# First queries' norms taken beside K's, paired bound rows, and one query product spread over the first scores of an attention and GEGLU block

## The chip, the cores and the metric

The kernel runs on one core of a Trainium2 chip. The metric is device time in microseconds (us) of one execution. An execution that the hardware profiler took lies beside the timed runs; its rows are what is read below. Times in rows count from the first instruction of the span.

The engines are called as in the profile: PE is TensorE's matmuls and PEld its weight loads, DVE is VectorE, ACT is ScalarE, POOL is GpSimd, SP is SyncE. A q behind a name (SPq, ACTq) marks the issuing of a DMA.

## What is computed

One transformer block over 2048 tokens of width 512. There are 32 query heads of width 16, and all of them share one K and one V head. All arrays are float32.

```python
def _A_ref(x, wq, wk, wv, wo):
    q = (x @ wq).reshape(B, S, H, Dh).transpose(0, 2, 1, 3)
    k, v = x @ wk, x @ wv
    scores = einsum("bhqd,bkd->bhqk", q, k) * (Dh ** -0.5)
    o = einsum("bhqk,bkd->bhqd", softmax(scores), v)
    return o.transpose(0, 2, 1, 3).reshape(B, S, H * Dh) @ wo
def _B_ref(x, w_gate, w_up, w_down):
    return (gelu(x @ w_gate) * (x @ w_up)) @ w_down
h = x + _A_ref(layernorm(x), wq, wk, wv, wo)
return h + _B_ref(layernorm(h), w_gate, w_up, w_down)
```

## The kernel before

**Precision.** Every float32 factor of a projection is split into a high and a low part (`split`), and a product is three matmuls: high by high, high by low, low by high. A score uses the same idea inside one matmul: its contraction has 50 rows, which are 16 rows of K's high part, 16 and 16 of the other combinations, and two rows that carry an upper bound of the score. The bound replaces the row maximum of the softmax.

**Blocks.** The tokens are four blocks of 512 (`T`). A block's queries are four chunks (`c`) of 128 columns, that is 8 heads each. A projection of one chunk, `pq_<block>_<chunk>`, is 12 matmuls of 128 x 512 in one PSUM bank. Attention runs over block, group of 4 heads (`g`) and 16 key chunks of 128 tokens (`kc`). A key chunk has two steps, counted by `n`: each step is one pair of score matmuls (two heads, on the upper and the lower 64 rows of PE) into a two-bank tile `s`, and one exponential `p` of 128 x 1024 on ACT. After both steps of a key chunk `weigh` multiplies `p` with V into `acc`; that is 4 matmuls in the program, which the trace shows as 8.

**Prologue.** It normalizes and transposes x, projects K and V for all four blocks (`project_k`), and starts on block 0's queries. Chunk 0 (`q_first`) is finished early, since the first group of heads needs it; chunks 1 to 3 (`q_rest`) are a generator of 36 matmuls that `advance` moves on by a number of matmuls. K's largest norm `k2m` comes from four small products `pkn` with a reduction each on DVE (`norm_k`, `max_k`). The queries' norms `pqn` come from one product, which DVE copies to `qn` and reduces. From `k2m` and the queries' norms POOL works out two factors (`mm`), ACT makes the bound `m`, and `first_bound` sends its rows to `qg_first`.

**The first queries' tile.** `qg_first` holds the 4 heads of the first group twice: on rows 0 to 49 and on rows 64 to 113. `first_q` brings the half that the first eight steps use, from DRAM (`q_d`). `fill_first` brings the crossed half on POOL's queue. The crossed half is first used at step 8 (`START`), where score matmuls begin to run beside half-array matmuls of the next blocks' projections and so swap sides.

**K's low part and V.** For each block ACT copies K and V out of PSUM (`add_k`, `leave_k`, which makes `vT`), POOL subtracts to get K's low rows (`low_k`), PE transposes V (`turn_v`) and DVE copies it into place (`leave_v`). `vT` and the plain copies of a query product, `pq_raw`, share one tag with 3 buffers.

**Order.** PE, POOL and ACT run in the order in which the code is written, in attention as in the prologue; so does DVE in the prologue and up to the last projection, and SP from `first_bound` on. Each engine is strictly in order. So a query product that is written in front of the first scores is done in front of them, and a copy that waits holds up what is written behind it on its engine. `HURRY` lists the chunks that are first copied out of PSUM as they are (`pq_raw`) and split later.

**After step 8.** Each stretch of steps is interleaved with the projections of blocks 1 to 3 (`later_q`), with the splitting of the dense weights on POOL (`part_weights`), and later with the output projection and the GEGLU products (`dense`, `weave`). The order of all that is fixed by step numbers.

Of the kernel before, what the change touches and what calls it, by code (L numbers as in the profile page):

```python
# [9 lines left out]
F32 = mybir.dt.float32  # L10
# [30 lines left out]
HURRY = ((0, 3), (1, 0), (1, 1))  # L41
# [21 lines left out]
def kernel(  # L63
# [104 lines left out]
    def run(outer, first):  # L168
# [20 lines left out]
        if first:  # L189
            eb = early.enter_context(tc.tile_pool(name="early", bufs=1))  # L190

            xT = {}
            for b in range(1, NB):
                for w in ("hi", "lo"):
                    if (b, w) in IN_RING:
                        part = ring_tile(f"xT_{w}_{b}").rearrange("p f i d -> p (f i) d")
                    else:
                        part = eb.tile([P, DC, T], F32R, name=f"xT_{w}_{b}")
                    xT.setdefault(b, []).append(part)
            wq_hi = eb.tile([P, DC, D], F32R, name="wq_hi")  # L200
            wq_lo = eb.tile([P, DC, D], F32R, name="wq_lo")
            sel = eb.tile([P, DC, H], BF16, name="sel")
            k2m = eb.tile([H, 1], F32, name="k2m")


        def project_q(b, cs, eng, col, whole=None):
# [6 lines left out]
            for c in cs:  # L213
# [134 lines left out]
        def first_q():  # L348
# [3 lines left out]
            for a in range(2):  # L352
                for r0, r1 in ((3 * DH + 1, KR), (0, 3 * DH)):
                    nc.sync.dma_start(
                        qg[64 * a + r0 : 64 * a + r1, a::2, :].bitcast(F32),
                        view[r0:r1, a:4:2, :T].bitcast(F32),
                    )
            return qg

        def fill_first(qg):  # L360

            view = q_d.rearrange("h r s -> r h s")
            for r0, r1 in ((0, 3 * DH), (3 * DH + 1, KR)):
                for a in range(2):
                    nc.gpsimd.dma_start(
                        qg[64 * a + r0 : 64 * a + r1, 1 - a :: 2, :].bitcast(F32),
                        view[r0:r1, 1 - a : 4 : 2, :T].bitcast(F32),
                    )
            m = ms[0]
            for j in range(4):  # L370
                row = 64 * (1 - j % 2) + 3 * DH
                nc.gpsimd.dma_start(
                    qg[row : row + 1, j, :].bitcast(F32), m[j : j + 1, :].bitcast(F32)
                )

        def first_bound(qg):

            m = ms[0]
            for u in range(2):
                for a, eng in enumerate((nc.sync, nc.scalar)):  # L380
                    eng.dma_start(
                        qg[64 * a + 3 * DH : 64 * a + 3 * DH + 1, 2 * u + a, :].bitcast(F32),
                        m[2 * u + a : 2 * u + a + 1, :].bitcast(F32),
                    )
# [10 lines left out]
        if first:  # L395
# [3 lines left out]
            with order:  # L399
                qg_first = prologue(  # L400
                    psum1, xT, wq_hi, wq_lo, sel, k2m, q_first, q_rest, advance,
                    first_q, first_bound, fill_first, eb
# [671 lines left out]
        with tc.manual_schedule(engines={mybir.EngineType.SP, mybir.EngineType.DVE}):  # L1074
            parts = None
            if first:
                work = later_q()
                parts = part_weights(early.enter_context(tc.tile_pool(name="parts", bufs=1)))

            token, left, wo_due = None, 6 * (NB - 1) * DC * DC, True  # L1080
            while n < lead:
# [166 lines left out]
    def prologue(psum1, xT, wq_hi, wq_lo, sel, k2m, q_first, q_rest, advance, first_q, first_bound, fill_first, eb):  # L1248
        with ExitStack() as pro:
            sb = pro.enter_context(tc.tile_pool(name="pro", bufs=1))  # L1250
            xT[0] = [sb.tile([P, DC, T], F32R, name=f"xT_{w}_0") for w in ("hi", "lo")]
# [203 lines left out]
            advance(q_first, 2)  # L1455
# [4 lines left out]
            for b in range(NB - 2, NB):  # L1460
                add_k(b, pks[b])
                vTs[b] = leave_k(b, pks[b])
# [3 lines left out]
            with tc.manual_schedule(engines={mybir.EngineType.SP}):  # L1466
# [4 lines left out]
                fill_first(qg)  # L1471
                for b in range(2, NB):
# [94 lines left out]
```

## Time and profile before

| | us |
|---|---|
| median of 3 runs | 1411.42 |
| lowest and highest of them | 1409.36 and 1412.17 |
| the profiled execution | 1409.89 |
| its span | 1408.1 |
| PE busy in it | 1391.7 (99%) |
| ACT busy in it | 1041.2 (74%) |
| DVE and POOL busy in it | 552.7 (39%) and 189.4 (13%) |

A busy PE is no proof that PE is the limit, because matmuls are pipelined and their ends are modelled. What counts is the stage. The prologue ends and attention begins at about 51 us in the span, so the change lies in the stretch from about 38 to 61 us. The chain of waits, the timelines of single engines and the table by stretches show what ends last there.

### The profile page before, as it was taken

To read this page: it belongs to the slowest core of one execution; us is meant where nothing else is said; L and a number is where in the kernel's file an instruction comes from. 1 tells how busy PE (TensorE), PEld (TensorE's weight loads), DVE (VectorE), ACT (ScalarE), POOL (GpSimd) and SP (SyncE) were. 2 spreads that over 40 slices of the span, in tenths; PEclk is the share of its full clock that TensorE was granted. 3 is DMA by queue.
4 is the path that set the end of the run, shared out by engine and by line. 5 is a ranking of instruction groups with operands and counts; after the bars stand their busy time and mean duration, and the time that the engine had idled before them with its cause. 6 is when DMAs were issued, how large, how long until landed. Compare 5 with 4: busy or idle time off the path is not lost.

```text
span 1408.1 us, 25648 instructions
## 1 busy us (share of the span) xinstructions
PE 1391.7 (99%) x10646; PEld 782.7 (56%) x10646; DVE 552.7 (39%) x982; ACT 1041.2 (74%) x1149; POOL 189.4 (13%) x288
## 2 busy tenths in 40 slices
PE   8999999999999999999999999999999999999998
PEld 7433333335555555555555655555555555557886
DVE  7322323333342434333252433424352342427665
ACT  7699999996777787777787777777787777772000
POOL 6655565501000000000000000001000000002000
PEclk9999999999999999999999999999999999999999
DMA  4578777842341322233252332223242241335551
GB/s 160 162 238 273 236 243 243 298 134 91 126 150 53 124 106 102 73 112 122 84 169 72 117 118 87 87 100 111 99 151 97 88 147 56 134 124 198 181 199 59
DMA packets 85041, 194.52 MB, mean 138 GB/s; under 512 B 9904, under 2 KB 24240, under 8 KB 84884
## 3 DMA queue, kind: packets, MB, share of 16 engines
q1 hardware_dynamic: 77484, 167.39, 35.3%
q0 software_dynamic: 7264, 25.30, 5.0%
q8 instruction: 86, 1.41, 0.4%
q14 instruction: 39, 0.32, 0.1%
q10 hardware_dynamic: 168, 0.10, 0.0%
HBM read 142.93 MB, written 49.55 MB: 137 GB/s over the span
## 4 chain that ended last, share of the span: by engine, by line
PE 93%; ACT 3%; DMA 1%; issue 1%; DVE 1%; POOL 0%; SPq 0%; ACTq 0%; DVEq 0%; POOLq 0%
PE acc L439 33%; PE s L431 19%; PE pu L949 9%; PE pg L949 8%; PE pd L949 4%; PE pq L429 4%; PE pd L626 3%; ACT p L435 3%; PE pd L648 3%; PE pg L648 3%; PE pu L648 3%; PE pp L626 2%; PE pp L757 1%; DMA x<-in_A_x_dram 1%; PE pxt L693 1%
## 5 line engine op out<-in xcount | busy, mean ns | idle before, releaser
L435 ACT ACTIVATE p<-s 128x1024 f32<-128x1024 f32 x1024 | 969.7, 1030 | 224.6 <-PE s L431 220.1
L439 PE MATMUL acc<-p,v_sb 128*32 128x512 f32 x4096 | 496.4, 600 | 0.0
L431 PE MATMUL s<-qg,kaug 50*128 50x512 f32 x1984 | 416.3, 423 | 3.7 <-ACT p L435 3.6
L431 PEld LDWEIGHTS s<-qg,kaug 50*128 50x128 f32 x1984 | 194.6, 184 | 217.8 <-ACT p L435 120.6
L439 PEld LDWEIGHTS acc<-p,v_sb 128*32 128x32 f32 x4096 | 109.8, 109 | 229.2 <-issue 226.0
L949 PE MATMUL pu<-x2h,w 64*128 64x512 f32 x672 | 211.8, 391 | 0.0
L949 PE MATMUL pg<-x2h,w 64*128 64x512 f32 x672 | 211.5, 391 | 0.1
L949 PEld LDWEIGHTS pu<-x2h,w 64*128 64x128 f32 x672 | 115.8, 185 | 15.1
L949 PEld LDWEIGHTS pg<-x2h,w 64*128 64x128 f32 x672 | 116.2, 185 | 12.6 <-DVE g L823 0.5
L949 PE MATMUL pg<-x2l,w 64*128 64x512 f32 x336 | 122.2, 391 | 0.0
L949 PE MATMUL pu<-x2l,w 64*128 64x512 f32 x336 | 121.8, 390 | 0.0
L826 ACT ACTIVATE ga<-ga 128x512 f32<-128x512 f32 x56 | 35.3, 634 | 89.2 <-DVE ga L821 89.2
L139 POOL TENSOR_SCALAR rstd<-mv 128x1 f32<-128x1 f32 x16 | 3.5, 221 | 666.4 <-DVE mv L137 666.4
L949 PE MATMUL pd<-w,gh 64*128 64x512 f32 x384 | 81.3, 392 | 0.0
L891 DVE TENSOR_TENSOR h<-h,pd 128x512 f32<-128x512 f32 x48 | 31.9, 685 | 115.4 <-PE pd L949 66.4
L1192 DVE SCALAR_TENSOR_TENSOR ga<-ga,g 128x512 f32<-128x512 f32 x70 | 48.3, 691 | 52.3 <-ACT ga L826 51.2
L452 DVE COPY oT<-acc 128x512 f32<-128x512 f32 x32 | 22.1, 692 | 112.1 <-PE acc L439 111.9
L479 DVE RECIPROCAL oc<-oc 128x128 f32<-128x128 f32 x64 | 56.3, 921 | 24.3 <-DMA oc<-acc_d 19.5
L810 DVE COPY g<-pg 128x512 f32<-128x512 f32 x56 | 38.8, 692 | 62.8 <-PE pg L949 57.0
L949 PEld LDWEIGHTS pu<-x2l,w 64*128 64x128 f32 x336 | 57.9, 185 | 7.6
L949 PEld LDWEIGHTS pg<-x2l,w 64*128 64x128 f32 x336 | 58.1, 185 | 6.1
L823 DVE SCALAR_TENSOR_TENSOR g<-g,pu 128x512 f32<-128x512 f32 x56 | 38.2, 683 | 40.4 <-PE pu L949 30.4
(248 smaller groups left out, 1462.4 us busy)
## 6 DMA issues: line engine op xcount, KB each, us to landing
w<-w_d SPq DMA_DIRECT2D x112, 512.0 KB
w<-w_d SPq DMA_DIRECT2D x28, 1024.0 KB
qg<-q_d SPq DMA_DIRECT2D x46, 200.0 KB
q_d<-qh SPq DMA_DIRECT2D x32, 256.0 KB
wo<-wo_d SPq DMA_DIRECT2D x8, 1024.0 KB
acc_d<-oT SPq DMA_DIRECT2D x31, 256.0 KB
oc<-acc_d SPq DMA_DIRECT2D x124, 64.0 KB
w_d<-w_0b POOLq DMA_DIRECT2D x14, 512.0 KB, 7.6
```

Of the source, the lines that this page charges most:

```text
L429: step()
L431: nc.tensor.matmul(s[:, a, :], kaug[rows, kc * P : (kc + 1) * P], qg[rows, 2 * u + a, :], start=True, stop=True,)
L435: nc.scalar.activation(p[:, 2 * u : 2 * u + 2, :], s, AF.Exp, scale=SCALE)
L439: nc.tensor.matmul(acc[32 * j : 32 * j + 32, :], v_sb[:, kc, :], p[:, j, :], start=(kc == 0), stop=(kc == KC - 1), skip_group_check=True,)
L479: nc.vector.reciprocal(oc[:, 1, sl], oc[:, 1, sl])
L626: nc.tensor.matmul(banks[k], lhsT[rows], rhs[rows], start=(turn == 0 and i == 0), stop=(turn == 1 and i == n - 1), skip_group_check=True,)
L648: nc.tensor.matmul(bank, lhsT, rhs, start=(i == 0), stop=(i == len(ts) - 1))
L810: nc.vector.tensor_copy(g, pg)
L823: nc.vector.scalar_tensor_tensor(g, g, 0.5, pu, op0=ALU.mult, op1=ALU.mult)
L826: nc.scalar.activation(a, a, AF.Tanh, scale=GELU_A * GELU_C)
L949: nc.tensor.matmul(e["bank"], lhsT[rows], rhs[rows], start=i == 0 and not e["both"], stop=last and e["both"], skip_group_check=True,)
L1192: (soon or lazy).pop(0)()
```

## The change

Three things are moved and one form of transfer is changed.

First, `pqn` and its two DVE instructions go between the norm products of K's blocks 1 and 2. They stood between those of blocks 2 and 3. The transposes of V move too: block 1's goes in front of K's last norm product, and those of blocks 2 and 3 go behind chunk 1's product.

Second, the bound rows of `qg_first` go two heads at a time: one transfer on SP and one on ACT where there were two each, and two on POOL's queue where there were four. POOL's constant rows come with the first transfers of SP. On POOL the subtraction for K's block 2 now stands between the crossed half's queries and its bound rows.

Third, chunk 3's product of block 0 is put between the first scores: 3 matmuls after step 1, 6 after step 3, 3 after step 5. For that block 0's transposed x (`xT[0]`) moves to a pool of its own, which is closed after step 5; the pool for splitting weights opens there, too. Chunk 2 is now the one that ACT copies as it is, and DVE does its split and chunk 3's copy.

```diff
-HURRY = ((0, 3), (1, 0), (1, 1))
+HURRY = ((0, 2), (0, 3), (1, 0), (1, 1))
...
-                    if b == 0:
+                    if (b, c) == HURRY[0]:
                         nc.scalar.activation(raw, pq, AF.Copy)
                     else:
                         nc.vector.tensor_copy(raw, pq)
...
+        def bound_rows(qg, a, side, queue):
+            row = 64 * side + 3 * DH
+            queue.dma_start(
+                qg[row : row + 1, a::2, :].bitcast(F32), ms[0][a:4:2, :].bitcast(F32)
+            )
...
-            for u in range(2):
-                for a, eng in enumerate((nc.sync, nc.scalar)):
-                    eng.dma_start(
-                        qg[64 * a + 3 * DH : 64 * a + 3 * DH + 1, 2 * u + a, :].bitcast(F32),
-                        m[2 * u + a : 2 * u + a + 1, :].bitcast(F32),
-                    )
+            for a, queue in enumerate((nc.sync, nc.scalar)):
+                bound_rows(qg, a, a, queue)
...
-                if first and n == 2:
+                if first and n in (2, 4):
+                    advance(q_rest, 6)
+                if first and n == 6:
                     for _ in q_rest:
                         pass
+                    x0.close()
+                    parts = part_weights(early.enter_context(tc.tile_pool(name="parts", bufs=1)))
...
+                if c == 1:
+                    advance(q_first, 2)
             b = NB - 1
             ks = square_k(b, pks[b])
-            advance(q_rest, 3)
+            pv = turn_v(1, vTs[1])
+            add_k(b - 1, pks[b - 1])
+            vTs[b - 1] = leave_k(b - 1, pks[b - 1])
             max_k(b, norm_k(b, ks))
...
                 fill_first(qg)
-                for b in range(2, NB):
-                    low_k(b, vTs[b])
-                advance(q_rest, 12)
-                for b in range(1, NB):
-                    leave_v(b, turn_v(b, vTs[b]))
-                advance(q_rest, 3 * DC * (DC - FIRST_Q) - 21)
+                low_k(2, vTs[2])
+                for a in range(2):
+                    bound_rows(qg, a, 1 - a, nc.gpsimd)
+                low_k(3, vTs[3])
+                advance(q_rest, 6)
+                leave_v(1, pv)
+                for b in range(2, NB):
+                    leave_v(b, turn_v(b, vTs[b]))
+                advance(q_rest, 12)
```

What follows are the instructions as they stand on single engines; numbers behind a name tell its instances apart. On PE, before, chunk 3's product (`pq_3`) ends in front of the first six pairs of scores (`s`):

```order
L223 MATMUL pq_3_781<-xT_hi_106,wq_hi 128x512
L223 MATMUL pq_3_781<-xT_lo_107,wq_hi 128x512
L223 MATMUL pq_3_781<-xT_hi_106,wq_lo 128x512
L431 MATMUL s_0_816<-qg_first,kaug 128x512 x2
L431 MATMUL s_1_820<-qg_first,kaug 128x512 x2
L431 MATMUL s_0_834<-qg_first,kaug 128x512 x2
L431 MATMUL s_1_838<-qg_first,kaug 128x512 x2
```

On PE in the changed kernel chunk 2's product (`pq_2`) ends there, and chunk 3's first matmuls follow the second pair:

```order
L226 MATMUL pq_2_756<-xT_hi_101,wq_lo 128x512
L432 MATMUL s_0_788<-qg_first,kaug 128x512 x2
L432 MATMUL s_1_792<-qg_first,kaug 128x512 x2
L226 MATMUL pq_3_805<-xT_hi_101,wq_hi 128x512
L226 MATMUL pq_3_805<-xT_lo_102,wq_hi 128x512
L226 MATMUL pq_3_805<-xT_hi_101,wq_lo 128x512
L432 MATMUL s_0_810<-qg_first,kaug 128x512 x2
L432 MATMUL s_1_814<-qg_first,kaug 128x512 x2
```

Twelve matmuls of 128 x 512 have moved from in front of the first score to between the first and the seventh pair.

On POOL, before, the factors end, K's block 1 is subtracted, and all transfers of the crossed half are issued in one go, ahead of the subtractions of blocks 2 and 3:

```order
L299 TENSOR_SCALAR mm_0_677<-mm_0_677,k2m 32x1
L1379 TENSOR_TENSOR kaug<-vT_651,kaug 16x512 x2
L365 DMA qg_first<-q_d 48x2x512 x2
L365 DMA qg_first<-q_d 1x2x512 x2
L372 DMA qg_first<-m_0_678 1x16x32 x4
L1379 TENSOR_TENSOR kaug<-vT_688,kaug 16x512 x2
L1379 TENSOR_TENSOR kaug<-vT_691,kaug 16x512 x2
```

On POOL in the changed kernel:

```order
L302 TENSOR_SCALAR mm_0_671<-mm_0_671,k2m 32x1
L1382 TENSOR_TENSOR kaug<-vT_654,kaug 16x512 x2
L369 DMA qg_first<-q_d 48x2x512 x2
L1382 TENSOR_TENSOR kaug<-vT_690,kaug 16x512 x2
L377 DMA qg_first<-m_0_672 1x2x512 x2
L1382 TENSOR_TENSOR kaug<-vT_696,kaug 16x512 x2
```

Four short transfers are gone from POOL's queue, and the two that carry bound rows stand behind one subtraction more.

On ACT, before, between the bound `m` and the first exponential `p`:

```order
L323 ACTIVATE m_0_678<-qn_0_674,mm_0_677 32x512
L381 DMA qg_first<-m_0_678 1x16x32 x2
L127 ACTIVATE qh_2_772<-pq_2_738 128x512
L242 ACTIVATE pq_raw_3_794<-pq_3_781 128x512
L435 ACTIVATE p_815<-s_0_816 128x1024
```

On ACT in the changed kernel:

```order
L326 ACTIVATE m_0_672<-qn_0_668,mm_0_671 32x512
L377 DMA qg_first<-m_0_672 1x2x512
L245 ACTIVATE pq_raw_2_769<-pq_2_756 128x512
L436 ACTIVATE p_787<-s_0_788 128x1024
```

One transfer and one copy of 128 x 512 have left ACT in front of the first exponential; the copy that is left is chunk 2's. From step 8 on, the order of all engines is the same as before.

More of the change, by code (lines that the diff above doesn't have):

```diff
@@ L203, in run @@
             k2m = eb.tile([H, 1], F32, name="k2m")
+            x0_pool = x0.enter_context(tc.tile_pool(name="x0", bufs=1))
+            xT[0] = [x0_pool.tile([P, DC, T], F32R, name=f"xT_{w}_0") for w in ("hi", "lo")]
         def project_q(b, cs, eng, col, whole=None):
@@ L1245, in run, with prologue @@
         late.close()
-    def prologue(psum1, xT, wq_hi, wq_lo, sel, k2m, q_first, q_rest, advance, first_q, first_bound, fill_first, eb):
+    def prologue(psum1, xT, wq_hi, wq_lo, sel, k2m, q_first, q_rest, advance, first_q, first_bound, fill_first, bound_rows, eb):
         with ExitStack() as pro:
             sb = pro.enter_context(tc.tile_pool(name="pro", bufs=1))
-            xT[0] = [sb.tile([P, DC, T], F32R, name=f"xT_{w}_0") for w in ("hi", "lo")]
             warm = sb.tile([P, 1], F32, name="warm")
```

31 lines of the change are left out of this document (12 added, 19 removed).

## The prediction

> **What bounds the kernel now.** I read the page first, then the table by stretches, then the chain of waits and each engine's timeline around the first scores. The page says that PE is the end of almost everything:
>
> ```profile
> PE 93%; ACT 3%; DMA 1%; issue 1%; DVE 1%; POOL 0%; SPq 0%; ACTq 0%; DVEq 0%; POOLq 0%
> ```
>
> The change touches only the stretch up to the seventh pair of scores, so the question is what ends last there, and whether time won there reaches the end. Two long stretches answer the second part (columns: PE, PEld, DVE, ACT, POOL busy, PE's clock, DMA share, GB/s):
>
> ```profile
> 61.00:300.00 239.00, 238.91 (x1815) 90.21 (x1817) 68.73 (x95) 234.71 (x252) 124.78 (x156) 1.00 0.76 244
> 300.00:1400.00 1100.00, 1095.79 (x8529) 651.72 (x8522) 443.36 (x794) 765.57 (x835) 24.38 (x50) 1.00 0.33 115
> ```
>
> From 61 to 300 us ACT is busy 234.71 of 239 us with exponentials, after that PE is. The order there doesn't change and both engines work without a gap worth naming, so what the start wins or loses is carried to the end one for one. PE's chain around the start:
>
> ```profile
> 46.83 3.51 PE pq L223 x15
> 50.43 0.61 ACT pq_raw L242
> 51.08 0.58 PE s L431 x2
> 55.44 1.86 PE acc L439 x8
> 58.45 1.86 PE acc L439 x8
> 64.89 1.00 PE acc L439 x8
> ```
>
> The first score starts at 51.08, behind 15 matmuls of block 0's queries and an ACT copy of the last. ACT's timeline of the same place:
>
> ```profile
> 45.78 0.81 ACT L323 ACTIVATE m<-qn,mm 32x512 fp32r<-32x512 f32 x1 [2.00 <-POOL mm L299]
> 46.62 1.22 ACTq L381 DMA_DIRECT2D qg_first<-m  x2
> 50.43 0.60 ACT L242 ACTIVATE pq_raw<-pq 128x512 f32<-128x512 f32 x1 [1.86 <-PE pq L223]
> 51.73 5.61 ACT L435 ACTIVATE p<-s 128x1024 f32<-128x1024 f32 x6 [0.71 <-PE s L431]
> 58.07 1.94 ACT L435 ACTIVATE p<-s 128x1024 f32<-128x1024 f32 x2 [0.73 <-PE s L431]
> 61.02 18.91 ACT L435 ACTIVATE p<-s 128x1024 f32<-128x1024 f32 x20 [1.01 <-PE s L431]
> ```
>
> ACT is to run exponentials back to back from 51.73 on, 18.91 / 20 = 0.945 us apart, but waits twice for PE: 0.73 and 1.01 us, 1.74 in all. Why PE is late shows in the stretches of 3.41 us (PE busy, its clock):
>
> ```profile
> 46.55:49.96 3.41, 3.41 (x18) 1.00 0.10 14
> 49.96:53.37 3.41, 1.91 (x10) 1.00 0.67 188
> 53.37:56.79 3.42, 2.94 (x12) 0.50 0.54 171
> 56.79:60.20 3.41, 3.41 (x16) 0.50 0.52 191
> 60.20:63.61 3.41, 3.41 (x32) 1.00 0.76 255
> 19.24:22.65 3.41, 2.58 (x15) 1.00 0.03 10
> ```
>
> ```profile
> 51.08 1.03 PE L431 MATMUL s<-qg_first,kaug 50*128 50x512 f32 x6 [0.75 <-ACT pq_raw L242]
> 52.81 0.50 PE L431 MATMUL s<-qg_first,kaug 50*128 50x512 f32 x2 [0.70 <-ACT p L435]
> ```
>
> The two rows of PE's timeline show its idle time in brackets, 0.75 and 0.70 us. After a stretch in which PE was busy 1.91 of 3.41 us, its granted clock is 0.50 for 6.83 us, and the same eight `acc` matmuls take 1.86 instead of 1.00 us.
>
> **The change, part by part. When the first score starts.** Three things must be done for it. First PE: 12 of the 15 matmuls leave; 3.51 / 15 = 0.234 each, so 2.81 less. The last now ends at 46.83 + 3.51 = 50.34; it would end at 47.53, and with ACT's copy (0.09 to start, 0.60, 0.05 to the score) the score could start at 48.27.
>
> Second POOL: the copy `pq_raw` takes the third `vT` buffer in turn, which is that of K's block 1, so it waits until POOL has done that block's subtraction:
>
> ```profile
> 45.12 0.62 POOL L299 TENSOR_SCALAR mm<-mm,k2m 32x1 f32<-32x1 f32 x1
> 45.82 2.61 POOL L1379 TENSOR_TENSOR kaug<-vT,kaug 16x512 fp32r<-16x512 f32 x2
> 48.38 2.42 POOL L365 DMA_DIRECT2D qg_first<-q_d  x4
> 50.79 1.96 POOL L372 DMA_DIRECT2D qg_first<-m  x4
> 52.82 5.29 POOL L1379 TENSOR_TENSOR kaug<-vT,kaug 16x512 fp32r<-16x512 f32 x4
> ```
>
> That ends at 48.43 now, and today nobody waits for it. With 0.65 for the copy and the step to PE it allows 49.08. The K norms bring it forward a little:
>
> ```profile
> 41.09 0.59 ACT L1356 ACTIVATE ks<-pk 16x512 bf16<-16x512 f32 x1 [2.19 <-PE pk L1349]
> 42.07 0.67 DVE L285 TENSOR_REDUCE q<-qn 32x1 f32<-32x512 f32 x1
> 42.67 0.67 DVE L1365 TENSOR_REDUCE k<-pkn 32x1 f32<-32x512 f32 x1
> 44.77 0.26 POOL L296 TENSOR_SCALAR mm<-mm 32x1 f32<-32x1 f32 x1
> ```
>
> K's last reduction (42.67) stands right behind the queries' (42.07, 0.67 long). With that one gone earlier, it waits for its own product alone. That product hardly moves: the queries' product, now ahead of K's last ones, delays `ks`, and chunk 1's three matmuls no longer stand before it. I take 0.18 us. At most 0.55 comes, if the last factor also takes 0.25 as its neighbour's 0.26, not 0.62; at least nothing. So POOL allows 48.9 (48.5 to 49.1).
>
> Third the bound rows: issued at 46.62 now. For the flight of such a transfer no row here has an end. The nearest is that of a later 64 KB transfer of SP with a waiting reader:
>
> ```profile
> 305.49 1.71 SPq L465 DMA_DIRECT2D oc<-acc_d  x4
> 309.09 3.39 DVE L479 RECIPROCAL oc<-oc 128x128 f32<-128x128 f32 x4 [4.56 <-DMA oc<-acc_d]
> ```
>
> From the end of issue to the reader are 309.09 - 307.20 = 1.89 us. A single issue is 1.22 / 2 = 0.61 us, so the rows land by 46.62 + 0.61 + 1.89 = 49.12, less 0.18, at the latest near 48.9; 4 KB should not take longer than 64. Halving the transfers saves one issue on each queue, and none of that is on the path: both first issues start at 46.62. I price it at nothing; if two descriptors fly longer than sixteen, up to 0.4.
>
> All three meet near 48.9. **First score at 48.9 instead of 51.08: 2.2 us** (1.7 to 2.8).
>
> **What PE does then.** ACT's first exponential starts 0.65 later, at 49.55; if ACT never waits, the ninth starts 8 x 0.945 = 7.56 later, at 57.1, where today it starts at 61.02. PE has to keep up: until the ninth pair it has eight pairs, 12 query matmuls and two `weigh`. Two pairs in a row are 0.66 (below), so 2.64; the matmuls 2.81 and about 0.2 at each of three changes of kind; the two `weigh` at full clock 2.00.
>
> ```profile
> 68.00 0.66 PE s L431 x4
> 60.31 0.43 PE pq L429
> ```
>
> That is 8.05 us, to 56.95; half a microsecond for the ninth pair among its query matmuls (the first of such is 0.43) and 0.1 to ACT give 57.5. So PE, not ACT, ends last by some tenths. I take 57.4: **the ninth exponential 3.6 us earlier** (3.0 to 4.4), which is the 2.2 plus 1.4 of the 1.74 that ACT waits now. This asks that the clock stays up. The query matmuls, free today only because they stand in front, cost nothing here as long as ACT has exponentials to do; if that cover were gone they would cost their 2.81.
>
> **Where transfers could be late.** From the ninth pair on, scores read the crossed half. Its bound rows now stand behind one subtraction more: 48.25 + 2 x 0.6 + 2.65 (half of 5.29) = 52.1 for the first, issued 1.3 later than now (50.79). The landing times of POOL's queue (KB, us to landing):
>
> ```profile
> qg_first<-q_d POOLq DMA_DIRECT2D x2, 192.0 KB, 4.3
> qg_first<-q_d POOLq DMA_DIRECT2D x2, 4.0 KB, 5.7
> qg_first<-m POOLq DMA_DIRECT2D x4, 2.0 KB, 6.6
> DMA to landing us min/median/max: 3.5/5.9/7.0
> ```
>
> They grow with each transfer queued in front, not with size. The new ones have only the two large ones in front, issued 2.65 us before, so I take 3.5 to 4.3: 55.6 to 56.4, ahead of the need at 56.95. By the maximum, 7.0, they land at 59.1 and cost 2.1.
>
> Here the Trainium skill speaks against the change: "DMA: Bandwidth & Descriptors", section "Rules for kernel authors", wants a slowest dimension that 16 divides, as a smaller one confines a transfer to fewer engines. The new rows are 1x2x512, the old 1x16x32. By that rule each row would ride on one engine and wait for all that is queued there, which leads to the rival of late rows below. The trace has a 1x2x512 transfer in the 4.0 KB row, and its 5.7 isn't above the 6.6 of the sixteen-part rows.
>
> Everything else is off the path. DVE's split of chunk 2 and copy of chunk 3 come while DVE waits for transfers. SP's load of the second group's queries moves ahead of chunk 3's stores; it is read at step 32. The weights' splitting on POOL starts about 3 us earlier, as do its readers.
>
> The sum against the profiled execution: 1409.89 - 3.6 = 1406.3. The median of the runs is 1411.42, 1.53 higher, so 1407.8.
>
> **The rivals.** *The clock still drops.* PE idles from 47.5 to 48.9, 1.4 us, a new gap. If it falls into one stretch, PE is busy about 2.0 of 3.41: near the 1.91 that brought the drop, below the 2.58 of 19.24 that did not. Against it: today's thin stretch holds at least two gaps and, after 50.34, only score pairs, the new one is full on both sides, and the stretch's border may cut the gap. Half clock for 6.83 us takes 3.4 us of PE work, all of it from the 3.6: gain 0.2 to 2, take 1.0; median 1410.4.
>
> On this the Trainium skill, "TensorE: Matmul & The Clock Gate", section "Why this matters for your kernels", allows gaps up to about 3 us before the clock drops. By that this rival can't happen; the trace disagrees, since no gap before 53.37 was longer than 0.75 us. The rival keeps its chance.
>
> *The crossed rows are late*, by the median 5.9 or the maximum 7.0: ACT waits 1.0 to 2.1 us at the ninth pair, gain 1.5 to 2.6; median 1409.4.
>
> *Slower.* The new gap brings the clock down, and it stays down. Today two stretches at half clock follow one thin one, although PE is busy 2.94 and 3.41 us in them. Each costs 1.71 us of PE work while PE is what ends last, so two eat the gain up and from the fourth on the kernel is slower: 4 x 1.71 - 3.6 = 3.2 us, median 1414.6. No row has more than two.
>
> That the change doesn't do what it says can be left aside: the order of the instructions shows it done.
>
> **How the numbers follow.** A measurement of this kernel tells 0.2%, 2.8 us, from no change. The forecast, 3.0 to 4.4 us of gain, has 0.55; the clock drops, 0.20; late rows, 0.13; slower, 0.12. Faster by over 0.2%: 0.54, as the scatter of the runs (2.8 us from lowest to highest) can take a little of the first and give a little of the third. Slower: 0.12. The rest, 0.34, is within. The predicted time is 1407.8. The range reaches from a gain of 4.4 with a median 1 us lucky, 1406.0, to the other two gains with a scatter of 0.8 above 1410.4, 1411.2; it leaves out the slower case.
>
> **What would show it.** Right: first score near 48.9, copy `pq_raw` starting as POOL's first subtraction ends, granted clock 1.00 from 46 to 64, exponentials without a gap of over 0.5 us before the ninth, and it near 57.4. Wrong: a 0.50 stretch near 50 to 60, the ninth pair waiting for `qg_first`, a first score after 49.5, or a later stretch that eats the gain.

## The result: the first scores start as forecast, and the kernel is slower

The changed kernel takes 1414.38 us (median of 21 runs, 1408.73 to 1416.87). The kernel before takes 1410.38 us beside it (median of 21, 1408.53 to 1413.57). The ratio is 1.0023 (95% interval 1.0016 to 1.0031). The profiled execution took 1414.91 us with a span of 1413.2, against 1409.89 and 1408.1. The forecast was 1407.8.

ACT's timeline of the changed kernel at the place of the change:

```profile
45.27 0.81 ACT L326 ACTIVATE m<-qn,mm 32x512 fp32r<-32x512 f32 x1 [1.12 <-POOL mm L302]
...
48.33 0.60 ACT L245 ACTIVATE pq_raw<-pq 128x512 f32<-128x512 f32 x1 [2.24 <-POOL kaug L1382]
49.63 5.71 ACT L436 ACTIVATE p<-s 128x1024 f32<-128x1024 f32 x6 [0.71 <-PE s L432]
55.95 1.94 ACT L436 ACTIVATE p<-s 128x1024 f32<-128x1024 f32 x2 [0.61 <-PE s L432]
62.99 2.85 ACT L436 ACTIVATE p<-s 128x1024 f32<-128x1024 f32 x3 [5.11 <-PE s L432]
68.14 4.69 ACT L436 ACTIVATE p<-s 128x1024 f32<-128x1024 f32 x5 [2.29 <-PE s L432]
```

The first exponential starts at 49.63 instead of 51.73, so 2.10 us of the forecast 2.2 are there. The eighth still comes in time. Then ACT waits 5.11 us for PE, and the ninth starts at 62.99, where 57.4 was forecast and 61.02 stood before. Three exponentials later it waits another 2.29. Why PE is late shows in PE's own timeline:

```profile
57.07 0.50 PE L430 MATMUL pq<-xT_hi,wq_hi 64*128 64x512 f32 x1
61.77 0.76 PE L432 MATMUL s<-qg_first,kaug 50*128 50x512 f32 x1 [4.20 <-DMA qg_first<-m]
...
64.17 3.51 PE L440 MATMUL acc<-p,v_sb 128*32 128x512 f32 x16
```

and in the chain of waits:

```profile
51.33 1.57 POOL kaug L1382
52.90 8.73 DMA qg_first<-m
...
61.77 0.76 PE s L432
```

The ninth step's first score, the first that reads the crossed half, waits 4.20 us for the crossed bound rows. They are issued at 52.90, behind block 2's subtraction, and count as landed 8.73 us later. The second loss is the clock. The stretches of 3.41 us of the changed kernel (columns as before: PE, PEld, DVE, ACT, POOL busy, PE's clock, DMA share, GB/s):

```profile
46.93:50.34 3.41, 2.17 (x11) 1.18 (x9) 2.16 (x10) 1.30 (x2) 3.33 (x4) 1.00 0.26 45
50.34:53.75 3.41, 3.41 (x17) 1.88 (x16) 1.46 (x1) 3.41 (x5) 3.33 (x4) 1.00 0.71 232
53.75:57.17 3.42, 3.42 (x24) 0.97 (x23) 1.41 (x3) 2.81 (x4) 3.29 (x4) 1.00 0.57 190
57.17:60.58 3.41, 0.40 (x1) 0.08 (x1) 1.08 (x2) 0.72 (x1) 0.57 (x2) 1.00 0.82 186
60.58:63.99 3.41, 2.22 (x9) 1.58 (x9) 0.00 (x0) 0.99 (x2) 0.00 (x0) 0.50 0.91 257
63.99:67.41 3.42, 3.42 (x17) 0.59 (x16) 0.00 (x0) 1.86 (x3) 1.22 (x2) 0.50 0.70 238
```

The new gap before the first score (busy 2.17 of 3.41) did not lower the clock in this execution. The wait did: after a stretch with 0.40 us of work PE runs at half clock for 6.83 us, and 16 `acc` matmuls take 3.51 us. What this cost is then carried on. The same exponential in ACT's timeline before:

```profile
84.23 77.14 ACT L435 ACTIVATE p<-s 128x1024 f32<-128x1024 f32 x82 [0.18 <-PE s L431]
313.78 3.77 ACT L435 ACTIVATE p<-s 128x1024 f32<-128x1024 f32 x4 [0.44 <-PE s L431]
```

and after:

```profile
88.39 77.15 ACT L436 ACTIVATE p<-s 128x1024 f32<-128x1024 f32 x82 [0.19 <-PE s L432]
317.87 3.77 ACT L436 ACTIVATE p<-s 128x1024 f32<-128x1024 f32 x4 [0.44 <-PE s L432]
```

It is 4.16 us late at 84 and 4.09 late at 314. The last exponential of the kernel is 4.81 late, the span 5.1 longer.

### The profile page after: what moved, and what is told of

Its sections match the earlier page's. It is cut to its first block, busy times and chain, and to the rows that moved or that the text cites. A ratio compares the mean times of both kernels' runs of the same rounds, so it can differ in the third digit from the quotient of the medians.

```text
span 1413.2 us, 25638 instructions
## 1 busy us (share of the span) xinstructions
PE 1392.4 (99%) x10646; PEld 780.0 (55%) x10646; DVE 550.6 (39%) x984; ACT 1040.5 (74%) x1148; POOL 187.7 (13%) x284
## 4 chain that ended last, share of the span: by engine, by line
PE 92%; ACT 4%; DVE 1%; POOL 1%; DMA 1%; issue 1%; SPq 0%; DVEq 0%; ACTq 0%; POOLq 0%
PE acc L440 33%; PE s L432 18%; PE pu L950 8%; PE pg L950 8%; PE pd L950 5%; PE pq L430 4%; PE pd L627 3%; ACT p L436 3%; PE pd L649 3%; PE pg L649 3%; PE pu L649 3%; PE pp L627 2%; PE pp L758 1%; PE pxt L694 1%; DMA qg_first<-m 1%
```

## The experiments

Each kernel was timed beside the kernel before, in five rounds. "Shift" is the start of the 33rd exponential against the row at 84.23 above; it sums up what the early stage won (negative) or lost in the profiled execution. Theories A to C are named in the first expectation, D in the second. The medians are of 6 to 12 runs, that of the changed kernel of 21. A shift is one execution's: "before, one ahead" has the early stage of the kernel before and still reads -0.97, as half clock lasted 3.41 us there and not 6.83.

| kernel | shift, us | median, us | lowest and highest | ratio to before, 95% |
|---|---|---|---|---|
| changed | +4.16 | 1414.38 | 1408.73, 1416.87 | 1.0023 (1.0016 to 1.0031) |
| four rows | +4.18 | 1415.94 | 1414.74, 1416.55 | 1.0030 (1.0018 to 1.0042) |
| rows ahead | -3.22 | 1408.63 | 1406.88, 1416.56 | 0.9984 (0.9970 to 0.9999) |
| rows ahead again | -3.23 | 1409.50 | 1406.88, 1411.78 | 0.9988 (0.9976 to 0.9999) |
| load behind stores | +2.51 | 1410.18 | 1408.92, 1414.25 | 0.9995 (0.9983 to 1.0007) |
| rows on SP and ACT | -3.22 | 1413.68 | 1408.17, 1417.43 | 1.0012 (0.9997 to 1.0026) |
| ahead and load behind | -3.20 | 1409.73 | 1407.11, 1414.19 | 0.9998 (0.9988 to 1.0009) |
| spread alone | -0.98 | 1409.05 | 1407.51, 1413.17 | 0.9987 (0.9977 to 0.9998) |
| spread alone again | -2.01 | 1408.87 | 1407.97, 1414.46 | 0.9989 (0.9975 to 1.0003) |
| norms and rows alone | -0.49 | 1411.73 | 1409.44, 1414.47 | 1.0005 (0.9995 to 1.0015) |
| loads earlier | -3.23 | 1412.59 | 1409.49, 1417.82 | 1.0018 (1.0008 to 1.0027) |
| weights one ahead | -1.72 | 1411.23 | 1408.05, 1417.33 | 1.0007 (0.9993 to 1.0021) |
| before, one ahead | -0.97 | 1409.66 | 1408.46, 1415.60 | 0.9996 (0.9987 to 1.0005) |
| changed, one ahead | +2.74 | 1415.19 | 1412.70, 1419.56 | 1.0039 (1.0024 to 1.0054) |
| wait filled | +0.91 | 1413.84 | 1412.33, 1416.23 | 1.0028 (1.0015 to 1.0040) |

### Form: four rows in the old form at the new place

```diff
-            queue.dma_start(
-                qg[row : row + 1, a::2, :].bitcast(F32), ms[0][a:4:2, :].bitcast(F32)
-            )
+            heads = [slice(a, 4, 2)] if queue is not nc.gpsimd else [slice(a, a + 1), slice(a + 2, a + 3)]
+            for hs in heads:
+                queue.dma_start(qg[row : row + 1, hs, :].bitcast(F32), ms[0][hs, :].bitcast(F32))
```

> The changed kernel with GpSimd's crossed bound rows sent as four transfers of one row again (16x32 elements each), at the same place behind the products of block 2's low rows. Theory A (the DMA engines are busy: a transfer is over when the last of the engines that carry it has got past what was queued on it, and the second group's load, 2 x 400 KB issued from 52.48, and the stores of the query rows are queued there): four rows meet the same queues; the first ninth-step product still waits 3.5 to 5 us for the crossed rows, the time stays within 1.5 us of the changed kernel (1414.4). Theory B (place: the rows are issued at 52.90, behind block 2's low rows, and so land late whatever else moves): the same, perhaps 1 us worse, as two more issues stand in the queue. Theory C (form: two rows of 2 KB in whole packets are slower than 16 pieces): the rows land in under 6 us, the wait falls under 1 us, and the time to 1409 to 1411.

The chain of waits of this kernel:

```profile
52.84 9.58 DMA qg_first<-m
...
62.55 0.76 PE s L432
```

The old form lands 9.58 us after issue, later than the 8.73 of the changed kernel. So the two-row form is not what makes the rows late, and theory C falls. The rule that the prediction quoted from the Trainium skill, "DMA: Bandwidth & Descriptors", "Rules for kernel authors", on transfers confined to fewer engines decides nothing here: at this place sixteen parts per row were no faster.

### Place: the rows ahead of block 2's subtraction

```diff
-                low_k(2, vTs[2])
                 for a in range(2):
                     bound_rows(qg, a, 1 - a, nc.gpsimd)
+                low_k(2, vTs[2])
                 low_k(3, vTs[3])
```

> The changed kernel with its two crossed transfers (two rows each) issued ahead of block 2's low rows, right behind the two 48-row transfers, so at about 49.7 and 50.2 instead of 52.9 and 53.4. Theory B (place): they land 8.7 us after issue at the latest, by 58.5, more likely 55.5 to 57 right behind the 48-row transfers (54.1 and 55.0); the wait at the ninth step falls from 4.2 to 0 to 1.5 us, TensorE's clock stays at full speed there, and the time falls by 3 to 6 us to 1408.5 to 1411.5. Theory A (busy engines): also better, since the rows stand ahead of the second group's load in the queues; the wait 0 to 1.5. Theory C (form): the landing stays near 8.7 us after issue, 58.4, a wait of 1 to 1.5 us. Theory D (TensorE's thin stretch from 50 to 60 lowers the clock anyway, the wait is not what costs): the clock still falls near 60, and the time stays within 1.5 us of 1414.4.

ACT's timeline with the rows ahead:

```profile
49.57 5.70 ACT L436 ACTIVATE p<-s 128x1024 f32<-128x1024 f32 x6 [0.71 <-PE s L432]
55.88 20.81 ACT L436 ACTIVATE p<-s 128x1024 f32<-128x1024 f32 x22 [0.61 <-PE s L432]
```

and the ninth step's first score in PE's:

```profile
57.00 0.50 PE L432 MATMUL s<-qg_first,kaug 50*128 50x512 f32 x1
```

The wait is gone. The ninth exponential, third of the 22, starts at 55.88 + 2 x 20.81 / 22 = 57.77. This kernel's landings, from the profile's DMA issues (KB, us to landing):

```profile
qg_first<-q_d POOLq DMA_DIRECT2D x2, 192.0 KB, 6.1
...
qg_first<-m POOLq DMA_DIRECT2D x2, 4.0 KB, 5.8
```

So moving two transfers 3.3 us forward turns a shift of +4.16 into -3.22, and the time falls below that of the kernel before. The completion events of the trace show how. A transfer on POOL's queue reports 16 times, and its reader waits for the last. For the first crossed transfer these times are:

```
changed      55.67 to 56.26 (eight)   57.75 58.29 58.30 58.50 59.58 60.89 60.92 61.64
rows ahead   52.68 to 53.04 (eight)   54.18 54.38 54.39 54.85 54.87 55.00 55.44 55.50
load behind  55.63 to 56.22 (eight)   57.73 58.16 58.17 58.22 58.51 58.80 59.29 59.57
```

Eight reports come within 3.5 us of issue in each kernel. The other eight are what is late. In the changed kernel they are awaited while the DMA share in the stretches above goes from 0.57 to 0.82 and 0.91; the rows ahead are through before that. The third row belongs to the next experiment.

### Traffic: the second group's load behind chunk 3's stores again

```diff
-                if kc == 2 and b * NG + g + 1 < NB * NG:
+                if kc == (2 if b or g else 3) and b * NG + g + 1 < NB * NG:
```

> The changed kernel with the load of the second group's queries (2 x 400 KB) behind the stores of chunk 3 on SyncE's queue again, as it stands in the kernel before; the crossed rows stay as changed, issued at 52.9. Theory A (busy engines, the load above all): the crossed rows land at 56 to 58, the wait at the ninth step is under 1 us, the time 1408.5 to 1411. Theory B (place): the rows still land 7 to 9 us after issue, the wait stays 3 to 4.5 us, the time within 1 us of 1414.4. The second group's load is needed only some 30 us later and costs nothing in either.

The chain of waits, and below it the stretch in which the clock falls:

```profile
52.84 6.73 DMA qg_first<-m
...
59.70 0.76 PE s L432
```

```profile
60.00:64.00 4.00, 4.00 (x21) 1.84 (x23) 0.00 (x0) 2.85 (x3) 1.88 (x2) 0.50 0.64 229
```

In this execution the rows land 6.73 us after issue, in that of the changed kernel 8.73. Other executions show that not all of the difference need be the load's: with the load ahead of the stores the same rows took 8.45 us (changed, one ahead) and 7.99 (wait filled), with the load behind them 7.44 (norms and rows alone). So the load costs about 0.6 to 2.0 us of the landing, and most of the flight stays without it. A wait of 2.2 us stays too, and in this execution half clock follows it; at 1414.25 us it is the slowest of the 12. The median, 1410.18, lies in the range of theory A, but the landing and the wait lie in neither. Place and load both count. What else holds the rows, the stores on SP's queue or POOL's own weight loads issued behind them, no run separates.

### The clock: the wait filled with work

```diff
                 if first and n == START:
+                    idle = psum1("idle")
+                    for k in range(16):
+                        nc.tensor.matmul(
+                            idle, wq_hi[:, 0, :P], xT[1][0][:, 0, :], start=(k == 0), stop=(k == 15)
+                        )
                     token = next(work)
```

> The changed kernel with 16 products more in front of the ninth step's first score (the same 128x512 product of block 1 again, into a bank that nobody reads, some 3.7 us at 0.23 us each): they keep TensorE at work while it waits for the crossed rows and compute nothing that is used. If half clock follows from the idle wait: no fall to 0.50 near 60 to 67; the rows land as late as in the changed kernel, the ninth exponential starts at 62.5 to 63.5 as there, but the thirteenth comes 2 us earlier than there (at 67, not 69), and the time falls by about 2 us, to 1412 to 1413. If the clock falls because of the thin stretch before the wait: the fall stays, the time stays at 1414 to 1415. If the 16 products end after the rows have landed they cost their overhang, under 1 us.

PE's timeline, ACT's, and the same stretches as above:

```profile
56.99 3.92 PE L1087 MATMUL idle<-xT_hi,wq_hi 128*128 128x512 f32 x16
...
61.19 0.47 PE L432 MATMUL s<-qg_first,kaug 50*128 50x512 f32 x1
...
62.51 1.92 PE L440 MATMUL acc<-p,v_sb 128*32 128x512 f32 x16
```

```profile
61.93 18.91 ACT L436 ACTIVATE p<-s 128x1024 f32<-128x1024 f32 x20 [4.11 <-PE s L432]
```

```profile
60.58:63.99 3.41, 3.35 (x28) 1.58 (x26) 0.00 (x0) 2.06 (x3) 0.00 (x0) 1.00 0.94 262
63.99:67.41 3.42, 3.42 (x30) 1.65 (x26) 0.00 (x0) 3.30 (x4) 1.89 (x2) 1.00 0.64 232
```

The rows are still late, but the clock stays at 1.00 and the same 16 `acc` matmuls take 1.92 us instead of 3.51. The shift is +0.91 instead of +4.16, 3.25 less. Of that, 0.58 is the first score's, which starts at 61.19 and not at 61.77, since the rows landed 0.8 us earlier in this execution. So some 2.7 us of the changed kernel's early loss are half clock, and half clock follows from the idle wait, not from the thin stretch before it. The median moved by only 0.5 us, where about 2 were expected. In this execution another 2.7 us were lost between the middle and the end, where the shift grew from +0.91 to +3.58 at the last exponential; the changed kernel lost 0.7 there. PE's timeline shows two waits in the dense layers at full clock, at which the shift grows by 0.9 and 1.4:

```profile
710.35 0.47 PE L950 MATMUL pu<-x2h,w 64*128 64x512 f32 x1 [0.48 <-DMA w<-w_d]
1035.62 0.46 PE L950 MATMUL pu<-x2h,w 64*128 64x512 f32 x1 [0.97 <-DVE gh L1201]
```

The profiled execution of the kernel before has neither. So the fill shows what half clock costs in the early stage, and not what it costs in the whole time.

### The parts alone

The spread alone is the kernel before with chunk 3's product between the first scores. Its bound rows are the old four transfers on each side, and its crossed rows stand ahead of block 2's subtraction.

```diff
...
-                if first and n == 2:
+                if first and n in (2, 4):
+                    advance(q_rest, 6)
+                if first and n == 6:
                     for _ in q_rest:
                         pass
...
```

> The kernel before with the third part of the change alone: chunk 3's product between the first scores, with its raw copies, pool and place of the second group's load; bound rows in four transfers of one row and K's norms as before, the crossed rows ahead of block 2's low rows. If the late crossed rows come from where the second part puts them (behind block 2's low rows): they are issued at about 50.8 and land by 57 to 58, the ninth step waits under 1 us, the first exponential starts at 50 to 50.6 instead of 51.73, and the time is 1407.5 to 1410. If they come from the load that the third part moves ahead of chunk 3's stores: the ninth step waits 2 to 4 us, the clock drops near 60, and the time is 1412 to 1415.

```profile
49.79 5.71 ACT L438 ACTIVATE p<-s 128x1024 f32<-128x1024 f32 x6 [0.71 <-DMA q_d<-m]
56.11 2.92 ACT L438 ACTIVATE p<-s 128x1024 f32<-128x1024 f32 x3 [0.61 <-PE s L434]
60.50 1.94 ACT L438 ACTIVATE p<-s 128x1024 f32<-128x1024 f32 x2 [1.48 <-PE s L434]
```

This is ACT's timeline. The first exponential starts at 49.79, only 0.16 later than in the changed kernel. So the third part brings nearly all of the earlier start by itself. PE waited 1.6 us for the crossed rows, between the two expectations, and the clock stayed up. The time, 1409.05, is the first one's. It ran a second time beside the second run of the rows ahead:

> The spread alone once more, unchanged, beside the rows ahead. It gains 1 us early (1.6 us of wait at its ninth step) and comes to the later groups 2 us later than the rows ahead: if late loads take the more the earlier a kernel comes to them, its runs scatter less, median 1408.8 to 1410, interval below 1 again.

In its profiled execution PE waited 0.6 us for the crossed rows this time, and the shift was -2.01. Nine of the 12 runs lay within 1407.97 to 1409.38. The median is in the expected range, but the interval holds 1.

The other half is the changed kernel with chunk 3's product in front of the first scores again:

```diff
...
-                if first and n in (2, 4):
-                    advance(q_rest, 6)
-                if first and n == 6:
+                if first and n == 2:
...
```

> The changed kernel without the third part: chunk 3's product stands in front of the first scores again, with the second group's load behind its stores; the first queries' sums beside K's and the two-row transfers stay, the crossed ones behind block 2's low rows. The first score starts 0.2 to 0.6 us earlier than before (51.08), the ninth step is due near 60. By busy engines alone: the crossed rows land 4.5 to 6 us after 52.9, by 59, no wait, 1409.5 to 1410.9 (the kernel before 1410.9). By place: they land 8 to 9 us after 52.9, at 61 to 62, a wait of 1 to 2 us, 1411 to 1413.

Its first exponential started at 51.88, 0.15 later than before. The expected 0.2 to 0.6 us are missing: with chunk 3's product in front, PE's order ends last, not POOL. The rows counted as landed 7.44 us after issue at 52.21, and the ninth step waited 1.2 us for them. That flight lies between the two expectations, the wait and the median in the second. The norms and the paired rows gain nothing measurable alone.

### Does the early gain reach the end?

Four edits more keep the early stage of the rows ahead. The first takes the rows to SP's and ACT's queues:

```diff
             for a, queue in enumerate((nc.sync, nc.scalar)):
                 bound_rows(qg, a, a, queue)
+            for a, queue in enumerate((nc.sync, nc.scalar)):
+                bound_rows(qg, a, 1 - a, queue)
...
-                for a in range(2):
-                    bound_rows(qg, a, 1 - a, nc.gpsimd)
```

> The changed kernel with the crossed bound rows taken off GpSimd's queue: SyncE and ScalarE send them, two rows each, right behind the first heads' bound rows (at about 46.8), with the same form. Theories A and B: they land by 50 to 52; the ninth step's products then wait only for the 48-row transfers (55.0 in the changed kernel), the wait there is under 0.5 us, no clock drop near 60, and the time falls to 1406.5 to 1409, below the kernel before (1410.4) by 1.5 to 4 us. Theory C: the same, as the form costs at most 9 us from 46.8. Theory D (clock): a fall to half clock near 58 to 66 remains and the time stays at 1412 to 1414.

The early stage did as expected (shift -3.22), the time did not. The chain of waits of this kernel, 200 us later, and the two stretches around:

```profile
253.13 11.88 DMA qg<-q_d
...
265.14 0.51 PE s L434
```

```profile
262.02:265.43 3.41, 0.49 (x3) 0.32 (x4) 0.00 (x0) 0.34 (x1) 0.00 (x0) 1.00 0.78 272
265.43:268.84 3.41, 3.41 (x17) 1.50 (x18) 0.00 (x0) 2.67 (x3) 1.98 (x3) 0.50 0.72 248
```

PE waits 2.9 us for the queries of group eight, and half clock follows; the shift jumps from -3.3 to +1.6. SP issued that load at 252.76. In the kernel before it was issued at 249.55 and its reader came 3.2 us later, so the kernel that is ahead comes to the same load with less to spare. I called that theory E, and tried both edits together, then loads two steps earlier, then, without that, a change to what holds SP's queue up (both edits below are against the two together):

```diff
-                if kc == (2 if b or g else 3) and b * NG + g + 1 < NB * NG:
+                if kc == (2 if b else 0 if g else 3) and b * NG + g + 1 < NB * NG:
...
-AHEAD_W = 2
+AHEAD_W = 1
-                raw = pw.tile([P, D], F32, tag="w_raw", bufs=AHEAD_W + 2, name=f"{name}r")
+                raw = pw.tile([P, D], F32, tag="w_raw", bufs=AHEAD_W + 3, name=f"{name}r")
```

> Rows ahead (the two-row crossed transfers issued ahead of block 2's low rows) and the second group's load behind chunk 3's stores, together, in the changed kernel. Theory A+B (the crossed rows were late for both reasons, and nothing else is at stake): no wait at the ninth step, no clock drop there, as with the rows ahead alone; 1407.5 to 1409, the median within 1 us of the rows ahead alone (1408.6). Theory E (the gain of the first 60 us is lost again later, at whichever group's load comes late on SyncE's queue): single runs still scatter by some 5 us above the lowest, whatever the early stage does, and the median lies anywhere from 1408 to 1412.

> Rows ahead and second group's load behind chunk 3's stores, and the loads of block 0's later groups (third to eighth) issued two steps earlier in the program, so ahead of the store of the sums before on SyncE's queue, by some 1 to 2 us. Theory E (the gain is lost again where a later group's load comes late: the wait of 2.9 us at 262 for the load issued at 252.8 in the run with the rows on SyncE and ScalarE): that wait gets rarer, the median falls by 0.5 to 2 us against the two edits alone, to 1406.5 to 1408. Rival: the waits are ruled by how far SyncE's queue lags behind (it waits for GpSimd to free the weights' buffers), and two steps change nothing: within 0.7 us of the two edits alone.

> Rows ahead, second group's load behind chunk 3's stores, and the weights of the projection and the dense layers loaded one step ahead of their conversion instead of two (four buffers as before), so that SyncE's queue waits about one conversion, some 5 us, less for GpSimd before it gets to a query group's load. Theory E (what is won early is lost at a late load in half the executions): the loads of groups seven and eight are issued 3 to 6 us earlier than 250.8 and 268 to 270, the late waits go, the runs gather at 1406.5 to 1408.5 with a median below 1408.5. Rival (the scatter is not from the loads): the scatter stays, median 1409 to 1411. A second rival (GpSimd now waits for its weights, which come later): the conversions end later than the dense layer needs them, over 1412.

Both edits together gave six runs within 1407.11 to 1408.45 and six from 1411.00 to 1414.19, with nothing between. The granted clock of the whole execution parts them, too: 0.999 in each of the first six, 0.996 or 0.997 in the others. A clock 0.002 lower over 1410 us is, as an estimate, 5.6 us more at half clock, which would be one fall more in the slow six; where, these runs don't show. In other kernels time and clock go together less well: two runs of the loads earlier at 0.999 took 1412.15 and 1413.52. The profiled one of both edits was of the first kind. The loads two steps earlier made it worse; PE waited for the queries of the next block's first group at 293 (1.2 and 0.6 us), and half clock followed at 296. With the weights one ahead the two loads were issued at 251.00 and 274.52, no earlier than in the rows ahead (250.78 and 268.23), so this edit did not do what it was for. Its profile shows another loss, at the gap before the first score:

```profile
47.57:50.98 3.41, 2.17 (x12) 1.15 (x11) 1.89 (x5) 1.95 (x3) 3.33 (x6) 1.00 0.40 94
50.98:54.39 3.41, 3.41 (x12) 1.91 (x8) 0.00 (x0) 2.42 (x3) 3.26 (x3) 0.50 0.66 215
```

That is the first rival of the prediction: the same 2.17 of 3.41 us as in the changed kernel, and here the clock falls, for 3.41 us; the shift is -1.72 instead of -3.22. In the ten other executions with the same gap of 1.2 us it held. The two controls with the weights one ahead:

> The kernel before with the weights loaded one step ahead instead of two, nothing else. Theory E: the kernel before comes to its groups 3.2 us later and seldom waits there (most of its runs lie within 1409.5 to 1411), so the median moves by less than 0.8 us, with fewer runs over 1412. If it falls by 2 us or more, the loads cost the kernel before as much as the changed ones, and the early gain is not what uncovers them.

> The changed kernel with the weights loaded one step ahead instead of two, nothing else. Its loss lies at the ninth step (the wait of 4.2 us and half clock behind it), not at the later groups, to which it comes 4 us later than the kernel before: no change, within 1 us of 1414.4. If it falls to 1411 or less, the later groups' loads were part of its loss.

Neither median moved by more than 1 us, as expected. That the changed kernel's loss is not at the later groups its own trace shows: the shift is +4.16 at 84 us already. But the profiled execution of the kernel before with this edit, at 1415.60 the slowest of its 12, lost 5.9 us near 236, with waits of 0.9 and 1.4 us for a group's load and 6.83 us at half clock behind them. That load was issued at 227.47 there, in the kernel before at 217.60, so the edit itself can make a load late, and this control says little about the kernel before. Theory E is not shown as a rule. Last, the rows ahead again:

> The rows ahead once more, unchanged, on the same chip as the spread alone. If the early gain of 3.2 us reaches the end as a rule, the median is again below 1409 and the interval below 1; if the first measurement was luck, as four kernels with the same early stage (rows on SyncE and ScalarE, both edits, loads earlier, weights one ahead) had medians from 1409.7 to 1413.7, it is 1410 to 1413 with an interval that holds 1.

Twice its interval lies below 1, by 0.01% at the least; the median, 1409.50, is above the 1409 that was asked for. The rows ahead are the one edit of the changed kernel that beat both kernels, by about 1.7 to 2.3 us against the kernel before (0.12% and 0.16%). The spread alone is as fast (0.13% and 0.11%), though its second interval holds 1. Both are less than the 3.2 us won early. That late loads and chance falls of the clock take gains away is seen in single profiles of other kernels; the two of the rows ahead have neither. In the first of them the shift grows by 1.5 us, 1.1 of it near 709 us, where PE waits 0.67 us for weights of the dense layers. What decides in which execution, stays open.

## Why the prediction was wrong

- **First score.** Forecast 48.9, measured 48.98 (0.65 before the exponential at 49.63). POOL's subtraction and the copy behind it end last, as worked out: the copy starts at 48.33, forecast 48.25. Right. K's norms brought `m` from 45.78 to 45.27, 0.51 us, near the upper bound of 0.55 rather than the 0.18 taken; the last factor on POOL did take 0.26. The sum came out partly by luck: block 1's subtraction took 2.98 us and not 2.61, which gave the 0.33 us more from the norms back.
- **PE up to the ninth pair.** With the rows in time the ninth exponential starts at 57.77, a gain of 3.25 of the forecast 3.6, and the clock stays up from 46 to 64. Right, as the rows ahead show; the changed kernel never got there.
- **The landing of the crossed rows: the step that failed.** The prediction put it so: "They grow with each transfer queued in front, not with size. The new ones have only the two large ones in front, issued 2.65 us before, so I take 3.5 to 4.3". Measured 8.73, and for such rows on POOL's queue in no profiled execution under 5.5. Half of the reports do come within 3.4 us; the reader waits for the other half. The issue came late as well, at 52.90 and not 52.1, since block 2's subtraction took 3.26 us and not 2.65. What is queued in front doesn't set the flight: right behind the same two large transfers, 3.3 us earlier, it is 5.94, and in the changed kernel's place it is 6.73 to 7.44 without SP's load beside it. What makes up the rest stays open. The bound on the other side, the maximum of 7.0 us, came from the same rows of the kernel before, whose traffic the change itself moved.
- **"Everything else is off the path."** SP's load was looked at for its own reader alone, at step 32. What it does to transfers under way beside it was left out. Putting it back takes about 0.6 to 2.0 us off the landing.
- **The price of a wait.** The rival of late rows had the mechanism and the place, with 1.0 to 2.1 us of wait. It measured 4.20, and half clock behind it cost more, which was not in this rival's sum. Against the rows ahead the ninth step's first score starts 4.77 us later (61.77 and 57.00) and the shift is 7.38 us worse, so 2.6 us are left for half clock; the filled wait gave 2.7.
- **The clock at the new gap.** It held in the profiled execution of the changed kernel and in nine others with this gap, and fell in that of the weights one ahead. The rival's chance was real, and its price, 1.6 to 3.4 us off the gain, near: 1.5 there. "No gap before 53.37 was longer than 0.75 us" leaves out the start, where PE waited 1.53 us at 1.5 and 0.83 at 22.3; the point against the rule stands.
- **The slower rival** blamed half clock in a row behind the new gap. The sign came true by another cause, so that is luck. Nor did the clock stay down behind that gap: in the one execution where it fell, it was back after 3.41 us.
- **One for one to the end.** It held from 84 to 314 (4.16 and 4.09). Up to the last exponential the shift of the fifteen profiled executions in the table grew by 0.2 to 0.8 us in five, by 1.4 to 2.7 in seven, and by 4.2 to 6.7 in the three with a late load. All of that is against one execution of the kernel before, at 1409.89 faster than its median, so the growth is partly that execution's luck. The base had some, too: 1411.42 was the median of 3 runs, and that of 21 is 1410.38.

## What to carry over

A small transfer that must be in time is issued ahead of compute on its queue, whatever form it has; its flight is not a constant (5.5 to 9.6 us here) and grew with a load that another queue had under way, so a landing time from a trace is to be taken over only where that traffic stays. A change that moves a big load is to be weighed by what lands beside it, not only by its own reader. A wait on the matmul engine is priced with the half clock that may follow it: here 4.2 us of wait cost 7.4.

## What the runs showed of the hardware

- The clock falls after much shorter idle times than 3 us. The Trainium skill, "TensorE: Matmul & The Clock Gate", "Why this matters for your kernels", allows gaps of up to about 3 us. The trace agrees for the waits of 4.20 us and disagrees for those of 2.2 us (load behind stores) and 1.24 us (weights one ahead), which were followed by 6.83 and 3.41 us at half clock. Waits of 1.6 and 1.2 us (spread alone, norms and rows alone) were not. The work in a stretch of 3.41 us sorts most rows of the sixteen profiles, with the stretches laid at the clock's own changes and the last 20 us of each kernel left out. After 0.40, 0.49, 0.67, 1.02, 1.34 and 1.62 us of it the clock fell, above 2.19 it held. Between these it did either: it fell after 1.88, 1.91, 2.08 and 2.17, and held after 1.84 and 1.85 (spread alone, twice), after 2.06 (four rows) and, in eight executions, after 2.17 to 2.19. So no single bound comes out of these rows.
- In all ten of these falls full clock came back after the first whole stretch in which PE was busy all 3.41 us. After 0.74, 2.22, 2.51, 2.94 and 3.28 us it stayed at half for one stretch more, so half clock lasts 3.41 us in some rows and 6.83 in others.
- Of the 16 completion reports of a 4 KB transfer eight come 2.8 to 3.5 us after issue in the changed kernel, with the rows ahead and with the load put back; the last of the other eight comes 5.4, 2.5 and 3.4 us after these.
